# A fused attention and feed-forward kernel: the order of every engine's work taken from written-out lists, and copies and casts moved between VectorE, ScalarE and GpSimd

## The chip, the core and the metric

The kernel runs on one core of one Trainium2 chip. Its time is the device time of one execution in microseconds (us). The engines are TensorE (PE in the profile; its weight loads are PEld), VectorE (DVE), ScalarE (ACT), GpSimd (POOL) and SyncE (SP), whose queue issues nearly all DMAs here.

## What is computed

A recurrent attention (4 batches, 8 heads, 768 steps, head size 48) is followed by a feed-forward layer over its 3072 rows. Cut to what matters:

```
for t in range(S):
    state = alpha[:, :, t, :, None] * state + einsum('bhd,bhe->bhde', k[:, :, t], v[:, :, t])
    y[:, :, t] = einsum('bhd,bhde->bhe', q[:, :, t], state)
x = y.transpose(0, 2, 1, 3).reshape(B * S, H * D)      # 3072 x 384
h = x @ w_in                                           # 384 x 2048
r = maximum(h, 0)
out = (s * (r * r) + b) @ w_out                        # 2048 x 384
```

## The kernel before

**Tiling.** The 3072 rows are 24 blocks of 128 steps, six to a batch. Attention is done a block at a time in chunked form. Blocks 0 to 5 come in three pairs, loaded in 384 KB pieces (`load_pair`); blocks 6 to 23 are single, in 192 KB pieces (`load_block`). Each has four loads, a (alpha), q, k and v. Below, a7 means the a load of block 7. There are four pair-sized buffers for each of the four, so a load of block n waits until block n-8 has been used.

**Steps of a block.** Names ending in `_1` forms (st1_...) are those of single blocks, the others those of pairs.
- ln: ACT takes the logarithm of a; cum: PE sums it along the steps; exp: ACT makes the decay and its inverse.
- vcast: v to bf16 (L524 for pairs, L740 for single blocks). For pairs 0 and 1, PE also reorders v (V) and ACT copies it (Vcopy, L543).
- qb, kb: DVE multiplies q and k by the decays (L554, L562, L746).
- T: PE transposes them (8 instructions), and Tcopy copies the result from PSUM (128x1024 bf16, L582 or L584 for pairs, two copies a pair; L764 for single blocks). Blocks 13 to 23 have a DMA transpose in place of both (Tdma).
- KV: PE; then the state: sfirst (DVE, first block of a batch, two instructions, L618), or t1 (DVE, L626) and snew (POOL, two instructions, L633).
- A: PE (L658); mask: DVE (L672); y: PE (L689, L697); yevac: ACT (L791).
- yT: PE transposes y (3 instructions, L796), yTcopy puts it in place (L808 DVE, L810 ACT); or one DMA transpose (yTdma, L813).

**Feed-forward.** The blocks form groups of 1, 1, 2, 2, 2, 4, 2, 2, 2, 2, 4. There are 96 units of the first product, mm1(0) to mm1(95) (PE, L834), each 512 columns of PSUM, each followed by relu (ACT, L843) and square (DVE, L855). Units 0 to 7 belong to blocks 0 and 1 and have 12 matmuls each, units 8 to 23 to blocks 2 to 5 and have 6. The second product is 100 quads of four matmuls, mm2(0) to mm2(99) (PE, L867), four quads a block and eight half quads for the last block. The last quad of a block is followed by oevac (DVE) or, for blocks 0 to 5, by oscale (ACT) and obias (POOL), and by ostore (SP).

**Weights.** Four pieces of w_in (w0 to w3) and then four of w_out (o0 to o3), 768 KB each, pass through the same four staging tiles `wst`, and each is cast in two halves on ACT or POOL (`cast_w_in(i, e)`, `cast_w_out(i, e)`). So o0 can't be loaded before both halves of w0 are cast. DVE also sums the w_out pieces (colsum, L427 and L435) for the bias term.

**PSUM.** Two banks hold `a_ps`; six more are handed out step by step: at most three hold results of mm1, two those of mm2, and two each those of cum, T and so on.

**What sets the order.** Each step is told to a planner by `op(engine, duration, priority, function, ...)` with what it reads and writes. `Schedule.run` plays the steps forward with these planned durations: whenever an engine is free it takes the ready step of the lowest priority number, where the number has an offset per kind of step (`KIND`) and per block (`BLOCK`), and loads are ranked by the string `LOADS`. `emit` then writes the instructions in the order of the planned begins. On the chip, each engine works through its own instructions strictly in that order, and a step whose input is late holds up all that stands behind it. Gaps of PE that are planned before 36 us are filled with matmuls of zeros (`warm`, L1137).

**Who does what.** Small lists say it: `POOL_CASTS` and `WIN_CASTS` (halves of w_out and w_in cast on POOL, the rest on ACT), `POOL_V` (pairs whose v is cast on POOL), `DVE_YC` (yTcopy on DVE, the rest on ACT), `PE_T` and `PE_Y` (single blocks transposed by PE rather than by DMA), `N_ACT_T` (pairs whose first Tcopy is on ACT).

Of the kernel before, what the change touches and what calls it, by code (L numbers as in the profile page):

```python
# [15 lines left out]
UNIT = 1.62  # L16
# [4 lines left out]
POOL_CASTS = [1, 3, 5, 7]  # L21
CASTP = -400.0
W_HW = True
WIN_CASTS = [0, 2, 3, 5, 7]
A2 = [0, 1, 2, 5, 8, 9, 10]
POOL_V = [0, 1, 2, 4]
DVE_VC = [6]
DVE_YC = [0, 2, 4, 6, 7]
NIN = 4
PE_T = [6, 7, 8, 9, 10, 11, 12]  # L30
PE_Y = [6, 7, 8, 9, 10, 11, 13]
# [3 lines left out]
N_ACT_T = 1  # L35
# [3 lines left out]
KIND = {'bias_copy': 2.5, 'bias_mm': 0.0, 'bias_mul': 2.75, 'cast_w_in': 0.0, 'cast_w_out': -0.625, 'colsum_add': 0.75, 'colsum_fold': -10.75, 'colsum_part': 1.625, 'mm1': 0.0, 'mm2': 3.375, 'obias': -11.25, 'oevac': 0.0, 'oscale': 9.75, 'relu': 0.0, 'square': 0.0, 'st1_KV': 18.75, 'st1_T': 0.0, 'st1_Tcopy': -5.625, 'st1_cum': -3.375, 'st1_exp': 0.75, 'st1_ln': 20.875, 'st1_qb': -2.25, 'st1_vcast': 0.0, 'st_A': -8.625, 'st_A2': 0.0, 'st_KV': -16.625, 'st_T': -0.5, 'st_Tcopy': 0.25, 'st_V': 10.625, 'st_Vcopy': 11.0, 'st_bl': 0.125, 'st_blexp': 0.0, 'st_cum': 0.25, 'st_exp': 0.0, 'st_kb': -19.0, 'st_ln': -0.875, 'st_mask': 0.0, 'st_qb': 0.0, 'st_sfirst': 0.0, 'st_snew': 0.0, 'st_t1': -1.625, 'st_vcast': -1.75, 'st_y': 0.0, 'st_yT': -0.375, 'st_yTcopy': 6.125, 'st_yevac': 6.125}  # L39
BLOCK = [-7.0, 0.375, -15.875, -1.125, 2.625, -0.5, -14.75, 5.375, -21.25, 0.125, 0.0, 0.875, 0.0, 0.0, -2.875, -13.75, 1.0, 2.375, 1.25, 3.625, -3.125, 18.375, 1.125, 6.375, 0.75, -0.625, 0.0, -7.75, 0.625, -21.375, -0.5, 3.25, 2.375, 2.5, 9.25]  # L40

LOADS = 'o1 a0 a1 q0 k0 v0 k1 q1 w0 v1 w1 w2 w3 o0 a2 k2 q2 v2 o2 o3 a7 k9 a9 v6 v7 a6 k7 q9 q6 k6 a8 q14 k8 k10 a10 a11 q7 k20 q10 q8 v9 v8 q15 a12 q11 v17 v11 q13 v13 k11 v10 q12 q16 a14 v12 a13 k14 k12 k17 k15 q23 k13 a15 v15 k16 q20 v16 q18 a16 a21 v14 q17 v18 a17 v21 a19 v23 a18 k19 k21 k18 a22 a20 k22 v20 v19 q19 v22 q21 a23 q22 k23'


class Schedule:
# [11 lines left out]
    pool_busy = 0.0  # L57
# [11 lines left out]
    def op(self, eng, dur, prio, fn, *args, r=(), w=(), lat=0.1, dma=None, take=(), drop=None, blk=None):  # L69
        me = len(self.ops)  # L70
        prio += KIND.get(fn.__name__, 0.0)
        if blk is not None:
            prio += BLOCK[blk]
        deps = set()
        for x in r:
            if x in self.writer:
                deps.add(self.writer[x])
        for x in w:
            if x in self.writer:
                deps.add(self.writer[x])  # L80
            deps.update(self.readers.get(x, ()))
        for x in r:
            self.readers.setdefault(x, []).append(me)
        for x in w:
            self.writer[x] = me
            self.readers[x] = []
        if drop is not None:
            self.drops[drop] = self.drops.get(drop, 0) + 1
        self.ops.append((eng, dur, prio, fn, args, deps, lat, dma, take, drop))

    def run(self):
        n = len(self.ops)
        end = [None] * n
        begin = [None] * n
        left = [len(o[5]) for o in self.ops]
        users = [[] for _ in range(n)]
# [3 lines left out]
        free = {}  # L100
        ready = {}
        for i, o in enumerate(self.ops):
            free.setdefault(o[0], {"POOL": 6.9, "DVE": 4.5}.get(o[0], 0.7))
            ready.setdefault(o[0], [])
            if not left[i]:
                ready[o[0]].append((0.0, i))
# [4 lines left out]
        soft = 0.0  # L111
        queue = 4.0
        flying = []
        todo = n

        def since(u):
            a = 0.0
            for d in self.ops[u][5]:
                same = self.ops[d][0] == self.ops[u][0]
                x = end[d] + (0.0 if same and u_eng(u) == "PE" else self.ops[d][6])  # L120
                a = max(a, x + (0.0 if same and self.ops[d][7] is None else self.HOP))
            return a

        def u_eng(u):
            return self.ops[u][0]

        def may(b, i, at):
            return b or at > self.warm_until

        def start(a, i):  # L130
            take = self.ops[i][8]
            if not take:
                return a
            if held[take[0][0]] + len(take) > self.most[take[0][0]]:
                return None
            free_banks = sorted(v for b, v in idle.items() if may(b, i, max(a, v)))
            return max(a, free_banks[len(take) - 1]) if len(free_banks) >= len(take) else None

        while todo:
            best = None  # L140
            for e, items in ready.items():
                at = [(s, i) for a, i in items if (s := start(a, i)) is not None]
                if not at:
                    continue
                t = max(free[e], min(at)[0])
                _, i = min((self.ops[i][2], i) for s, i in at if s <= t + 1e-9)
                if best is None or t < best[0]:
                    best = (t, e, i)
            t, e, i = best
            ready[e] = [x for x in ready[e] if x[1] != i]  # L150
            eng, dur, _, _, _, _, lat, dma, take, drop = self.ops[i]
            begin[i] = t
            if dma is None:
                if eng == "DVE" and self.ops[i][3].__name__ in self.shared:
                    dur += 0.9 * min(dur, max(0.0, self.pool_busy - t))
                free[e] = end[i] = t + dur
                if eng == "POOL":
                    self.pool_busy = end[i]
            elif eng == "POOL":
                free[e] = t + dur  # L160
                at = max(t + 3.2, soft)
                soft = end[i] = at + 1.1 * dma + (1.2 if soft < at < queue else 0.0)
                flying = [x for x in flying if end[x] > at]
                for x in flying:
                    end[x] += dma
                queue = max(queue, at) + dma
                for e2, items in ready.items():
                    ready[e2] = [(since(x), x) for _, x in items]
            else:
                queue = max(t + self.LEADS.get(self.ops[i][3].__name__, 1.8), queue) + dma  # L170
                end[i] = queue
                flying.append(i)
                free[e] = max(t + dur, queue - self.AHEAD)
            for x in take:
                b = min(
                    (b for b in idle if may(b, i, max(t, idle[b]))), key=lambda b: (idle[b], -b)
                )
                del idle[b]
                self.bank[x] = b
                held[x[0]] += 1  # L180
            if drop is not None:
                until[drop] = max(until.get(drop, 0.0), end[i] + lat + self.HOP)
                drops[drop] -= 1
                if not drops[drop]:
                    idle[self.bank[drop]] = until[drop]
                    held[drop[0]] -= 1
            todo -= 1
            for u in users[i]:
                left[u] -= 1
                if not left[u]:  # L190
                    ready[u_eng(u)].append((since(u), u))
# [29 lines left out]
def kernel(  # L221
# [356 lines left out]
    def st_Tcopy(m, x):  # L578
        dst = qkT_of(m)[:, :, x].rearrange("a c u j -> a c (u j)")
        src = t_of(m, x).rearrange("a c u j -> a c (u j)")  # L580
        if x < 1 and m < N_ACT_T:
            nc.scalar.activation(out=dst, in_=src, func=AF.Copy)  # L582
        else:
            nc.vector.tensor_copy(out=dst, in_=src)  # L584
# [39 lines left out]

    def st_t1(n):
        nc.vector.tensor_tensor(  # L626
            out=t1_sb[n % 2], in0=p_of(n), in1=s_sb[(n - 1) % 4], op=ALU.add
        )

    def st_snew(n):  # L630
        for e in range(2):
# [3 lines left out]
                in0=t1_sb[n % 2][rows, :, cols],  # L635
# [103 lines left out]
    def st1_vcast(n):  # L739
        nc.gpsimd.tensor_copy(  # L740
            out=vb_sb[n // 2 % 2][:, n % 2],
            in_=block_in(v_in, n).rearrange("a h d -> a (h d)"),
        )
# [19 lines left out]
    def st1_Tcopy(n):  # L763
        nc.vector.tensor_copy(  # L764
            out=qkT1_of(n).rearrange("a x p t -> a (x p t)"),
            in_=t1_of(n).rearrange("a x p t -> a (x p t)"),
        )
# [197 lines left out]
    def pair_ops(pm):  # L965
# [40 lines left out]
        if pm < N_PAIR_T:  # L1006
            for x in range(2):
                tb = ("T", 2 * pm + x)
                op("PE", 0.46, t, st_T, pm, x, r=src[x], w=[tb], lat=0.27, take=[tb], blk=c0)
                eng, dur = ("ACT", 0.92) if x < 1 and pm < N_ACT_T else ("DVE", 0.6)  # L1010
# [13 lines left out]
    def state_ops(n, t, pb):  # L1024
        s0, s1 = ("S", (n - 1) % 4), ("S", n % 4)
        bl = ("bl", n // 2 % 2, n % 2)
        if n % NCH == 0:
# [35 lines left out]
    def block_ops(n):  # L1063
# [10 lines left out]
        op("POOL", 0.6, t, st1_vcast, n, r=[("v", *ii)], w=[("vb", *j)], blk=n)  # L1074
# [4 lines left out]
        if n in PE_T:  # L1079
            op("PE", 0.46, t, st1_T, n, r=qk, w=[("T", n)], lat=0.27, take=[("T", n)], blk=n)  # L1080
            op("DVE", 0.6, t, st1_Tcopy, n, r=[("T", n)], w=[("qkT", *j)], drop=("T", n), blk=n)
# [94 lines left out]
```

## Time and profile before

| | |
|---|---|
| median of 7 runs | 185.66 us (184.99 to 186.12) |
| profiled execution | 185.71 us, span 183.9 us |
| PE busy | 173.8 us (94%), 1807 matmuls |
| DVE busy | 138.6 us (75%) |
| ACT busy | 111.0 us (60%) |
| POOL busy | 55.0 us (30%) |
| DMA | 34.36 MB, mean 187 GB/s |
| first mm1 begins | 22.1 us |
| last matmul ends | 180.9 us |

The profiled execution's span lies 1.8 us under its own time; that time is within 0.05 us of the median. PE's busy time is no measure of what it gets done, since its ends are modelled: what counts is how far apart matmuls start. Back to back, a unit of mm1 takes 0.66 us, a quad of mm2 0.65 us, eight transposes 0.45 us.

### The profile page before, as it was taken

To read this page: it belongs to the slowest core of one execution; us is meant where nothing else is said; L and a number is where in the kernel's file an instruction comes from. 1 tells how busy PE (TensorE), PEld (TensorE's weight loads), DVE (VectorE), ACT (ScalarE), POOL (GpSimd) and SP (SyncE) were. 2 spreads that over 40 slices of the span, in tenths; PEclk is the share of its full clock that TensorE was granted. 3 is DMA by queue.
4 is the path that set the end of the run, shared out by engine and by line. 5 is a ranking of instruction groups with operands and counts; after the bars stand their busy time and mean duration, and the time that the engine had idled before them with its cause. 6 is when DMAs were issued, how large, how long until landed. Compare 5 with 4: busy or idle time off the path is not lost.

```text
span 183.9 us, 4689 instructions
## 1 busy us (share of the span) xinstructions
PE 173.8 (94%) x1807; PEld 123.0 (67%) x1807; DVE 138.6 (75%) x253; ACT 111.0 (60%) x237; POOL 55.0 (30%) x103
## 2 busy tenths in 40 slices
PE   7496899899999999999999999999999999999993
PEld 5274787677776778775455867877866687554572
DVE  6069959999999997899886583887879966356241
ACT  2582499769778548675857755688743165459100
POOL 7843749262064236410211272011232310000000
PEclk9969999999999999999999999999999999999999
DMA  4999999979999998999869997988993552201022
GB/s 98 264 310 347 391 361 259 325 175 212 191 219 248 215 212 185 218 208 214 220 135 198 215 174 178 228 176 178 183 218 95 118 150 46 87 2 43 4 86 87
DMA packets 111495, 34.36 MB, mean 187 GB/s; under 512 B 104432, under 2 KB 109936, under 8 KB 111472
## 3 DMA queue, kind: packets, MB, share of 16 engines
q1 hardware_dynamic: 111184, 34.06, 78.8%
q8 instruction: 14, 0.23, 0.5%
q14 instruction: 9, 0.07, 0.1%
q10 hardware_dynamic: 288, 0.00, 0.1%
HBM read 25.17 MB, written 4.72 MB: 162 GB/s over the span
## 4 chain that ended last, share of the span: by engine, by line
PE 64%; DVE 17%; SPq 7%; DMA 5%; issue 4%; ACT 1%; ACTq 0%; DVEq 0%
PE bank L867 28%; PE bank L834 26%; SPq L372 5%; DMA wst<-in_moe_w_in_dram 5%; DVE gt L855 4%; DVE qk L746 3%; PE a_ps L658 2%; DVE am L672 2%; PE bank L697 2%; DVE colsum L435 2%; DVE colpart L427 2%; SPq L399 2%; PE bank L689 1%; PE bank L778 1%; PE bank L713 1%
## 5 line engine op out<-in xcount | busy, mean ns | idle before, releaser
L867 PE MATMUL bank<-w_out_bf,gt 128*128 128x384 bf16 (+1 forms) x400 | 72.0, 319 | 0.4 <-DVE gt L855 0.4
L834 PE MATMUL bank<-xd,w_in_bf 128*128 128x256 bf16 (+2 forms) x528 | 71.1, 282 | 0.5 <-ACT binv L511 0.3
L843 ACT ACTIVATE r<-bank 128x512 bf16<-128x512 f32 x96 | 56.1, 600 | 24.6 <-PE bank L834 11.1
L834 PEld LDWEIGHTS <-w_in_bf 128*128 128x128 bf16 x528 | 46.2, 98 | 16.0 <-issue 0.8
L855 DVE TENSOR_TENSOR gt<-r 128x512 bf16<-128x512 bf16 x96 | 44.3, 475 | 16.6 <-ACT r L843 16.0
L867 PEld LDWEIGHTS <-gt 128*128 128x128 bf16 x400 | 36.2, 97 | 19.7 <-DVE gt L855 0.5
L740 POOL CAST vb<-v_in 128x384 bf16<-128x384 f32 x18 | 10.2, 571 | 49.3 <-DMA v_in<-in_v_dram 18.0
L633 POOL TENSOR_TENSOR s_st<-t,blast 64x192 bf16<-64x192 bf16 x32 | 19.3, 602 | 18.9 <-DVE t L626 15.9
L877 DVE SCALAR_TENSOR_TENSOR o_sb<-bank,s_col,bias_w 128x384 f32<-128x384 f32 (+1 forms) x19 | 11.3, 594 | 13.6 <-PE bank L867 13.5
L672 DVE TENSOR_TENSOR am<-a_ps,mask_one 128x1024 bf16<-128x1024 f32 x14 | 17.1, 1220 | 2.1 <-PE a_ps L658 1.9
L791 ACT ACTIVATE yn<-bank 128x384 bf16<-128x384 f32 x24 | 11.8, 493 | 11.2 <-PE bank L697 11.0
L728 ACT ACTIVATE b_s<-bank 128x384 f32<-128x384 f32 x18 | 8.9, 492 | 7.3 <-PE bank L718 6.4
L746 DVE TENSOR_TENSOR qk<-q_in,b_s 128x384 bf16<-128x384 f32 x18 | 12.1, 674 | 0.9 <-ACT b_s L728 0.8
L706 ACT ACTIVATE la<-a_in 128x384 bf16<-128x384 f32 x18 | 9.4, 521 | 2.2 <-DMA a_in<-in_alpha_dram 2.2
L746 DVE TENSOR_TENSOR qk<-k_in,binv 128x384 bf16<-128x384 f32 x18 | 10.4, 583 | 0.0
L626 DVE TENSOR_TENSOR t<-bank,s_st 128x384 bf16<-128x384 f32 x16 | 8.8, 549 | 1.5 <-PE bank L778 1.0
L901 POOL TENSOR_TENSOR o_sb<-o_sb,bias_w 128x384 f32<-128x384 f32 x6 | 6.3, 1059 | 9.4 <-DVE bias_w L461 6.2
L728 ACT ACTIVATE binv<-bank 128x384 f32<-128x384 f32 x18 | 8.9, 497 | 0.0
L1137 PE MATMUL bank<-zeros_bf 128*128 128x256 bf16 x36 | 7.4, 359 | 1.1 <-DVE zeros_bf L298 1.1
L697 PEld LDWEIGHTS <-am 128*128 128x128 bf16 x192 | 7.1, 96 | 1.6 <-DVE am L672 1.2
L658 PEld LDWEIGHTS <-qkT 64*128 64x128 bf16 x192 | 5.5, 94 | 3.4 <-issue 2.1
L689 PE MATMUL bank<-s_st,qkT 128*128 128x96 bf16 x80 | 6.7, 206 | 0.3 <-DVE xd L808 0.3
(84 smaller groups left out, 181.4 us busy)
## 6 DMA issues: line engine op xcount, KB each, us to landing
out_dram<-o_sb SPq DMA_DIRECT2D x23, 192.0 KB, 2.2
a_in<-in_alpha_dram SPq DMA_DIRECT2D x18, 192.0 KB, 3.8
k_in<-in_k_dram SPq DMA_DIRECT2D x18, 192.0 KB, 4.0
v_in<-in_v_dram SPq DMA_DIRECT2D x18, 192.0 KB, 3.8
q_in<-in_q_dram SPq DMA_DIRECT2D x18, 192.0 KB, 3.7
wst<-in_moe_w_in_dram SPq DMA_DIRECT2D x4, 768.0 KB, 8.6
wst<-in_moe_w_out_dram SPq DMA_DIRECT2D x4, 768.0 KB, 7.4
a_in<-in_alpha_dram SPq DMA_DIRECT2D x3, 384.0 KB, 6.2
```

The source lines that it names most:

```text
L633: nc.gpsimd.tensor_tensor(out=s_sb[n % 4][rows, :, cols], in0=t1_sb[n % 2][rows, :, cols], in1=blast(n)[rows].unsqueeze(2).to_broadcast([6 ...
L672: nc.vector.tensor_tensor(out=dst, in0=src, in1=mk.unsqueeze(1).to_broadcast([128, dst.shape[1], 128]), op=ALU.mult,)
L697: nc.tensor.matmul(out=y_of(n)[:, 48 * h : 48 * h + 48], lhsT=am_sb[n % 2][:, h % 2, h // 2, :], rhs=v[:, 48 * h : 48 * h + 48], start=(h ...
L728: nc.scalar.activation(out=(binv_sb if inv else b_sb)[n // 2 % 2][:, n % 2].rearrange("a h d -> a (h d)"), in_=cb[:, 0 : H * D], func=AF.E ...
L740: nc.gpsimd.tensor_copy(out=vb_sb[n // 2 % 2][:, n % 2], in_=block_in(v_in, n).rearrange("a h d -> a (h d)"),)
L746: nc.vector.tensor_tensor(out=qk1_of(n)[:, x, :, 0:D], in0=block_in((q_in, k_in)[x], n), in1=(b_sb, binv_sb)[x][n // 2 % 2][:, n % 2], op= ...
L791: nc.scalar.activation(out=yn_sb[n // 2 % 2][:, n % 2], in_=y_of(n), func=AF.Copy)
L834: nc.tensor.matmul(out=hp[:, i * n : (i + 1) * n], lhsT=w_in_bf[:, kk, 128 * j : 128 * (j + 1)], rhs=xd_sb[g % 3][:, kk, 0:n], start=(kk = ...
L843: nc.scalar.activation(out=r_sb[w % 2], in_=bank("h", w), func=AF.Relu)
L855: nc.vector.tensor_tensor(out=dst, in0=r, in1=r, op=ALU.mult)
L867: nc.tensor.matmul(out=bank("o", i)[:, cols], lhsT=gt_sb[:, slot, j, :], rhs=w_out_bf[:, j, cols], start=(j == 0), stop=(j == NJ - 1),)
L877: nc.vector.scalar_tensor_tensor(out=out_sb[i % NOUT][:, cols], in0=bank("o", i)[:, cols], scalar=s_col, in1=bias_w[:, cols], op0=ALU.mult ...
```

## The change

**The lists.** `KIND`, `BLOCK` and the choice by priority go. A dictionary `ORDER` holds, for each of the five engines, the numbers of all its steps (the number of a step is its place in the sequence of `op` calls) in the order in which the engine is to do them. `run` only walks the lists, gives out PSUM banks and works out the planned begins as before.

**Who does what:**

```diff
-POOL_CASTS = [1, 3, 5, 7]
+POOL_CASTS = [0, 1, 3, 5, 7]
-WIN_CASTS = [0, 2, 3, 5, 7]
+WIN_CASTS = [1, 4, 6]
-POOL_V = [0, 1, 2, 4]
-DVE_VC = [6]
-DVE_YC = [0, 2, 4, 6, 7]
+POOL_V = [0]
+ACT_V1 = [6, 17, 18, 22, 23]
+ACT_T1 = [6, 7, 8, 9, 10, 11]
+DVE_VC = []
+DVE_YC = [0, 2, 3, 8, 9, 10, 11]
-PE_Y = [6, 7, 8, 9, 10, 11, 13]
+PE_Y = [7, 8, 9, 10, 11, 13]
-N_ACT_T = 1
+ACT_T = [0, 2, 3, 4]
+ACT_S = [0]
...
+ORDER = {
+    "SP": """
+        31 35 34 32 33 37 36 38 3 0 6 9 39 12 40 16 42 41 21 26 43 351 47 211 45 44 46 49 48 395
...
+    "POOL": """
+        51 56 79 81 2 7 156 10 14 13 18 23 158 28 230 301 308 359 381 200 111 366 403 388 207
...
         for _ in range(n):
             best = None
-            for e, items in ready.items():
...
+            for e in engines:
...
+                i = lists[e][place[e]]
+                assert self.ops[i][0] == e
+                if left[i]:
+                    continue
+                a = max(known[i], free[e])
...
+    def st_scopy(n):
+        nc.scalar.activation(out=scratch(), in_=p_of(n), func=AF.Copy)
+
+    def scratch():
+        return out_sb[NOUT - 1].rearrange("a (p e) -> a p e", p=NP)
...
+        dst = vb_sb[n // 2 % 2][:, n % 2]
+        src = block_in(v_in, n).rearrange("a h d -> a (h d)")
+        if n in ACT_V1:
+            nc.scalar.activation(out=dst, in_=src, func=AF.Copy)
+        else:
+            nc.gpsimd.tensor_copy(out=dst, in_=src)
...
+        if n in ACT_T1:
+            nc.scalar.activation(out=dst, in_=src, func=AF.Copy)
+        else:
+            nc.vector.tensor_copy(out=dst, in_=src)
...
+        if n in ACT_S:
+            op("ACT", 0.37, t, st_scopy, n, r=[pb], w=[("os", NOUT - 1)], drop=pb, blk=n)
+            op("POOL", 1.2, t, st_snew, n, r=[("os", NOUT - 1), bl], w=[s1], blk=n)
+        elif n % NCH == 0:
```

In words: of the pair Tcopies, three more are on ACT (both of pair 1, one of pair 2); of the seven single ones, six (blocks 6 to 11) are on ACT and one stays on DVE. The first state of block 0 is no longer two DVE instructions but a copy on ACT (scopy) and two instructions on POOL. v is cast on ACT for pairs 1 and 2 and for blocks 6, 17, 18, 22 and 23, before on POOL. Of w_in, five halves are cast on ACT and three on POOL (before three and five), of w_out three and five (before four and four). Block 6's y is transposed by DMA instead of by PE. `LOADS`, `UNIT` and the priorities no longer decide anything. No other arithmetic is changed.

**The lists, translated** (from the step numbers; on the left the order in which the planner before emits, to the same point):

| engine | before | after |
|---|---|---|
| SP, loads | a0 a1 q0 k0 v0 k1 q1 w0 v1 w1 w2 w3 o0 o1 a2 k2 q2 v2 o2 o3, the DMAs of Vdma(2), a7 k9 a9 v6 v7 a6 k7 q9 q6 k6 | a0 a1 v0 q0 k0 k1 q1 v1 w1 w0 w2 w3 a2 o0 q2 o1 v2 k2 o2 o3 a6 a8 a7, those of Vdma(2), k6 q6 v6 k7 q7 a10 v7 k8 |
| DVE, from kb of pair 1 | kb(1) twice, Tcopy(0,1), sfirst(0), qb(1) twice, Tcopy(1,1), t1(1), mask(0), Tcopy(1,0), mask(1) in two halves, mask(2), yTcopy(0) | kb(1) twice, Tcopy(0,1), qb(1) twice, mask(0), mask(1) in two halves, t1(1), half of mask(3), yTcopy(0) |
| ACT, from the first Tcopy | Tcopy(0,0), Vcopy(0) twice, cast_w_in(0,1), yevac(0), Vcopy(1,0), yevac(1), cast_w_in(2,0), Vcopy(1,1), yevac(2), yTcopy(1), relu(0) | Vcopy(0,1), Tcopy(0,0), Vcopy(0,0), scopy(0), vcast(1), Tcopy(1,1), Tcopy(1,0), cast_w_in(1,0), yevac(0), cast_w_in(1,1), yevac(1), Vcopy(1,0), cast_w_in(0,0), Vcopy(1,1), yTcopy(1), cast_w_in(2,1), relu(1), relu(0) |
| PE, around the first units | y(0), A(2) and A(3), V(1,0), yT(0), y(1), V(1,1), y(2), yT(1), mm1(0), mm1(1), mm1(2), KV(1) | y(0), A(2) and A(3), y(1), V(1,0), yT(0), V(1,1), yT(1), KV(1), mm1(1), mm1(0), y(2), mm1(4), mm1(2) |
| PE, first transposes of single blocks | T(9) ahead of mm1(16), then T(6), T(7), T(10), T(8), T(11), T(12) | T(6) ahead of mm1(16), then T(7), T(8), T(9), T(10), T(11), T(12) |

Later in the lists, cum and ln of single blocks stand well ahead of where they were (cum(18) is 144th on PE, before 204th), and neighbouring mm1 units often swap places. The last 15 steps of PE are quads of mm2 in both.

## The prediction, made before the changed kernel was run

> **What bounds the kernel now.** I read the page first (parts 1, 2 and 4), then the chain of waits in order of time, then busy times by stretch, then the waits, then groups by line and form.
>
> ```profile
> PE   7496899899999999999999999999999999999993
> DVE  6069959999999997899886583887879966356241
> ACT  2582499769778548675857755688743165459100
> DMA  4999999979999998999869997988993552201022
> ```
>
> PE looks full nearly throughout, ACT has room, and DVE and DMA are near their limit in the first half. The chain says where the halves meet: until 61.7 us it is made of DVE steps (squares, qk products, column sums, masks), with the w_in loads before 22 us; from then to 180.9 it is PE alone.
>
> ```profile
> 61.70 0.84 DVE qk L746
> 62.59 0.62 PE bank L757 x8
> ...
> 170.43 10.45 PE bank L867 x80
> 180.91 0.42 DVE o_sb L877
> ```
>
> So the end is fixed by how much PE work is done by 62.6 us. By stretch (from:to, length; busy us of PE, PEld, DVE, ACT, POOL; clock, DMA share, GB/s):
>
> ```profile
> 8.80:22.10 13.30, 11.13 (x154) 8.31 (x153) 11.44 (x21) 6.90 (x16) 6.39 (x9) 0.87 1.06 345
> 22.10:62.60 40.50, 39.25 (x481) 30.34 (x478) 37.74 (x63) 32.54 (x72) 17.60 (x22) 1.00 0.99 250
> 62.60:180.90 118.30, 118.27 (x1146) 80.99 (x1146) 85.89 (x161) 68.17 (x145) 23.72 (x39) 1.00 0.72 152
> ```
>
> In 22.1 to 62.6 PE did 192 matmuls of L834, which are 24 units at 0.66 us (15.8), 68 of L867, 17 quads at 0.65 (11.1), and 221 of attention and bias, at their back-to-back pitch 10.6 us. That is 37.5 of 40.5 us: **3.0 us were lost** there. In the 118.3 us after it nothing that a wait row shows was lost. Before 22.1, the first units wait for their inputs. DVE was 93% busy in the middle stretch, ACT 80%.
>
> **The change, part by part.**
>
> *Copies from DVE to ACT.*
>
> ```profile
> L764 DVE COPY qkT<-bank 128x1024 bf16<-128x1024 bf16 x7 | 4.8, 680 | 0.2 <-PE bank L757 0.2
> L582 ACT ACTIVATE qkT<-bank 128x1024 bf16<-128x1024 bf16 x1 | 1.1, 1119 | 0.0
> ```
>
> Nine copies (three of pairs, six of single blocks): DVE loses 9 x 0.68 = 6.1 us, ACT gains 9 x 1.12 = 10.1. The Trainium skill speaks against such a move: "ScalarE: Activation LUTs", in its rules for kernel authors, says to use VectorE for simple elementwise work, up to about three times as fast in bf16. By that, the nine would cost ACT 9 x 3 x 0.68 = 18.4 us, and ACT would reach 133 us from this edit and the next. The row says 1.65 times for this very tile, read from PSUM. I take the row.
>
> *The rest.* DVE also loses sfirst(0) (2 x 0.35) and gains two yTcopies net (2 x 0.34): minus 6.1 us in all, 138.6 to 132.5. ACT gains scopy (0.49, as the Vcopy of that shape), two pair casts of v (2 x 0.85, nearest row ln of that shape at 844 ns), five single ones (5 x 0.52, ln at 521), one w half net (0.85), and loses three yTcopies (1.5): plus 4.1, so 111.0 + 10.1 + 4.1 = 125 us. POOL loses two pair casts (1.8), five single ones (2.9) and one w half net (0.8), and gains snew(0) (1.2): minus 4.3. So although one more half of w_out is cast there, GpSimd casts 22 tiles instead of 30. PE loses three transposes (0.17 us); SP gains one DMA transpose.
>
> *POOL against DVE.* The "SBUF" page of the Trainium skill ("SBUF — State Buffer", the rule on the shared port pair) says a DVE step with two SBUF inputs and a GpSimd step that reads SBUF exclude each other for the whole instruction. In this trace the 65 squares with no POOL work beside them took 0.42 us, the 31 with some 0.59. By the rule 4.3 us less on POOL could free up to 4.3 us of DVE; by the trace, where DVE lost some 10 us (31 x 0.17 on squares, 11 x 0.26 on L746, the rest on L554 and column sums) to 46 us of POOL work, 1 us. I take 1; the end doesn't hang on it once DVE is relieved.
>
> *Head start.* Ahead of yTcopy(0), which mm1(0) needs, DVE does from 12.64 us on (start to start) before: kb 0.95, Tcopy 0.60, sfirst 0.71, qb 0.95, Tcopy 0.60, t1 0.47, mask 1.13, Tcopy 0.60, masks 1.20, mask 1.13: 8.3, so at 21.1. After: without the sfirst, two Tcopies and mask(2), but with half of mask(3): 5.9, so from 18.6. ACT then decides. Vcopies, Tcopies, scopy and vcast, 5.0 us from 11.7 on, are done before w1 comes: the casts of w0 and w1 began at 16.7 and 20.0, one pair piece and w1 apart; after, w1 is loaded ahead of w0 and behind that pair piece, so it lands some 1.4 us behind the old w0, at 18.1. From there cast 0.75, yevac(0) 0.38, cast 0.75, yevac(1) 0.38, yT(1) 0.3 and KV(1) 0.5 put mm1(1) at 21.1, and mm1(0), after its own cast, at 21.8. The first unit was at 22.1. By the pitches above, the lists have 7.8 us of PE work ahead of it before, 7.9 after: **1.1 us** gained. The bounds are 0 (casts on ACT late) and 2.4 (DVE's whole saving).
>
> *The stretch to 62.6.* Adding durations down the lists, DVE's work to the end of square(15) falls from 36.7 to 28.1 us: sfirst(0) and three Tcopies are gone (2.5), and behind it now stand a column sum, two adds and the fold, four qk products of later blocks, a yTcopy and a square (6.4), while one yTcopy (0.3) came ahead. It ended at 50.9. On ACT, work to relu(15) is 30.9 against 29.4; to relu(31) 61.5 against 47.9, which ended at 78.7, 31 us of it idle. ACT's first relu ends near 23.5, with 14.9 us of its list done; relu(31) then can't end before 70.1, 8.6 us ahead of what it was. So ACT has cover, if thin: 46.6 us of work in what was 55. Loads are the other limit, DMA share is 0.99. Before, the first T of a single block (T(9)) needed 12.6 MB of loads with 33.1 us of PE work ahead of it (its list at the pitches above); after, T(6) needs 12.0 MB at 31.8. That is 0.6 MB, 2.8 us at 212 GB/s, for 1.3 us of PE work: loads allow 1.5 us more lead, and for T(7), with as many loads as T(9) had, 35.4 - 33.1 = 2.3 us. So of the 3.0 us lost I take half back: **1.6 us**, bounds 0 and 3.0.
>
> *New waits.* v casts on ACT now stand ahead of relus; yTdma(6) stands on SP ahead of q10, k11, a14 and waits for yevac(6). It costs nothing if the loads issued before it (the queue runs some 4 us ahead of landing) last; else about 1 us of loads for T(10). bias_mm moves 17 places back on PE, and with it the first obias; behind that on POOL stands snew(8), due only at y(9). After 62.6 PE's order has lost its old zero of waits. For all this nothing in the trace gives a price; nearest are PE's own waits before (0.2 to 0.8 us each), bounds 0 and 3: I take two small ones, **0.7 us** lost; a gain is excluded, since PE loses nothing there now.
>
> *Tail.* The last mm2 quads, two evacuations and stores are as before: 0.
>
> Sum on the profiled execution: 185.7 - 1.1 - 1.6 - 0.2 + 0.7 = 183.5; its time equals the median within 0.05.
>
> **The rivals.**
>
> *Full gain* (0.15): ACT and loads both keep up, the 3.0 us vanish and nothing new comes: 185.7 - 1.1 - 3.0 - 0.2 = 181.4. For it: DVE's 8.6 us less by square(15). Against: DMA share 0.99 up to 62 us.
>
> *Slower: ACT's queue held by v* (0.26). In-order ACT has relus behind seven v casts.
>
> ```profile
> POOL vb L740 <- DMA v_in<-in_v_dram: 18.0, 8, 4.1
> ACT r L843 <- PE bank L834: 11.1, 19, 1.2
> ```
>
> On POOL 8 of 18 casts waited, 2.25 us each, hidden there since POOL was 30% busy. On ACT some three of the seven would wait: PE goes on for two units in free banks (1.3 us) and then stalls, 0.95 us each, 2.9 in all, while nothing of the 3.0 us comes back. It decides as soon as a v lands over 1.3 us after ACT reaches its cast. Time: 185.7 - 0.2 - 1.1 + 2.9 = 187.3. Against it: the loads are now in the order of the blocks, so v6 and v7 land with their own q and k.
>
> *No difference* (0.13): the loads set the pace, PE waits at T(6) to T(13) for what it gained, and the bound just changes its name: 185.7 - 0.2 = 185.5. For it: DMA at 0.99 to 1.06; against: the 0.6 MB above. That the change doesn't do what it says belongs here too: its casts on GpSimd fall, so no gain can come from more of them.
>
> **How the numbers follow.** Forecast 0.46 (183.5; own range 182.3 to 184.8), full gain 0.15, no difference 0.13, slower 0.26. A change under 0.3% (0.6 us) can't be told from none here. Faster: 0.46 + 0.15 = 0.61; same 0.13; slower 0.26. The range goes from just under the full gain, 181.2, to the slower rival's 187.3.
>
> **What would show it.** Right: first L834 matmul at 21 us; DVE under 90% in 22 to 62, ACT over 90%; the chain turning to PE alone some us earlier; PE's L867 and L834 without waits later; DVE 131 to 133, ACT near 125, POOL near 51 us. Wrong: ACT waiting on v_in with PE waiting on ACT r; PE waits after 62; SP waiting on yevac(6) with loads behind; or the first unit no earlier than 22.

## The result and the profile after

| | before | after |
|---|---|---|
| median | 185.65 us (34 runs) | 183.72 us (13 runs, 182.89 to 185.28) |
| profiled execution | 185.71 us, span 183.9 | 184.39 us, span 182.6 |
| first mm1 begins | 22.1 us | 21.27 us |
| last matmul ends | 180.9 us | 179.5 us |

The ratio of after to before is 0.9895, interval 0.9871 to 0.9919: 1.9 us faster, against a forecast of 183.5 us. Some executions of a kernel fall into a slower state: medians here are of all runs, ratios and their intervals of the others alone. The profiled execution of after is 0.7 us above its median. The changed kernel was run once more beside the last experiments (184.39 us where before took 186.41, ratio 0.9872 [0.9815, 0.993]); that run's profiled execution took 183.55 us, so I read both. Line numbers of after are 30 to 45 higher: mm1 L834 is now L874, mm2 L867 is L907, Tcopy L764 is L805 on ACT, vcast L740 is L781 on POOL and L779 on ACT; in the experiments they differ from these by one to three.

Busy time of after by engine, and its busy tenths in 40 slices, from the page:

```profile
PE 174.0 (95%) x1797; PEld 122.0 (67%) x1797; DVE 130.6 (72%) x244; ACT 120.1 (66%) x252; POOL 49.5 (27%) x97
...
DVE  6079748979699996989776697366896983454332
ACT  2578999979799879957976652846535056666200
...
DMA  4999999977899899999999989997985972000323
```

DVE's unbroken nines of before are gone, ACT's row is now the fuller one up to 60 us, and DMA has a seven and an eight at 41 to 50 us where it had nines. PE is busy for the same 174 us: it does the same work in a shorter span. By stretch, in the columns used before:

```profile
22.10:62.60 40.50, 39.62 (x498) 31.07 (x496) 33.72 (x60) 37.05 (x80) 15.65 (x21) 1.00 0.94 231
62.60:179.50 116.90, 116.52 (x1107) 78.56 (x1105) 82.11 (x158) 67.62 (x146) 22.13 (x36) 1.00 0.73 159
```

In 22.1 to 62.6 DVE went from 37.74 to 33.72 us, ACT from 32.54 to 37.05, and PE ran 498 matmuls in place of 481. The chain of waits, in order of time (start, us, what), turns to PE for good later than before:

```profile
43.34 4.71 DMA k_in<-in_k_dram
...
48.14 0.56 DVE qk L784
...
63.82 0.48 DVE qk L784
64.34 0.62 PE bank L795 x8
...
71.71 0.41 ACT la L742
72.12 0.50 ACT r L883
72.66 0.32 PE bank L749
```

The DVE stretch is shorter (8% of the chain, 17% before): it began near 27 us and now runs from 48.1, where a load of k lands, to 64.3. The loads ahead of it and SP, which issues them, are 23% of this chain (12% before), but 3% of the chain of after's second run, so nothing is built on that. A logarithm on ACT at 72 us stands in the chain as a new late step. And the waits of after (engine and line, what it waited for, us in total, times, longest):

```profile
POOL vb L781 <- DMA v_in<-in_v_dram: 38.0, 9, 11.6
...
ACT vb L779 <- DMA v_in<-in_v_dram: 1.8, 2, 1.1
...
PE bank L818 <- ACT vb L779: 0.5, 1, 0.5
PE bank L560 <- ACT yn L831: 0.5, 1, 0.5
```

The same kind of wait costs PE nothing here on POOL, where it adds up to 38 us, and 0.5 us of PE time on ACT, where it adds up to 1.8.

To see where the time came from I took, for each step of PE's list, its start minus the PE work that stands ahead of it in that list (at the back-to-back pitches). Before's value less a kernel's own is the kernel's lead:

| PE work done, us (time) | after | after, second run | h1, early DVE undone | h2 | h3 | e3 | e2 |
|---|---|---|---|---|---|---|---|
| 7.9, the first unit (21) | 1.0 | 1.4 | -0.5 | 0.4 | 1.3 | 0.6 | 1.1 |
| 20 (34) | 2.3 | 2.9 | 1.4 | 2.3 | 2.4 | 2.5 | 2.1 |
| 32 (47) | 2.3 | 2.9 | 1.4 | 2.3 | 2.4 | 1.9 | -0.9 |
| 42 (57) | 1.4 | 2.2 | 0.8 | 2.2 | 1.4 | 1.7 | -2.2 |
| 58 (75) | 1.1 | 2.1 | 0.0 | 1.7 | 1.2 | 1.8 | -6.6 |
| 160 (178) | 1.2 | 2.1 | -0.9 | 1.8 | -0.5 | 1.7 | -6.4 |

All of it is won before 34 us, and 0.8 to 1.2 us is given back between 47 and 75 us, in small waits. From there on the lead of after is constant. The profiled executions of h1 and h3 took 1.0 and 1.6 us more than their medians, so of their columns the early rows count.

Between the first unit and 34 us PE loses some 2.3 us in before and 1.0 in after, in small waits on several engines. The waits of 22 to 40 us name only 0.9 us of before's loss; here they are, and then all of after's:

```profile
PE bank L867 <- DVE gt L855: 0.4, 1, 0.4
PE bank L834 <- ACT binv L511: 0.3, 1, 0.3
PE bank L834 <- ACT r L843: 0.2, 1, 0.2
```

```profile
PE bank L836 <- ACT r L883: 0.2, 1, 0.2
```

### The profile page after: what moved, and what is told of

Its sections match the earlier page's. It is cut to its first block, busy times and chain, and to the rows that moved or that the text cites. A ratio compares the mean times of both kernels' runs of the same rounds, so it can differ in the third digit from the quotient of the medians.

```text
span 182.6 us, 4621 instructions
## 1 busy us (share of the span) xinstructions
PE 174.0 (95%) x1797; PEld 122.0 (67%) x1797; DVE 130.6 (72%) x244; ACT 120.1 (66%) x252; POOL 49.5 (27%) x97
## 4 chain that ended last, share of the span: by engine, by line
PE 61%; SPq 14%; DMA 9%; DVE 8%; issue 3%; POOL 1%; ACT 1%; ACTq 0%; POOLq 0%; DVEq 0%
PE bank L907 28%; PE bank L874 25%; DMA wst<-in_moe_w_in_dram 6%; SPq L402 5%; SPq L409 5%; DMA k_in<-in_k_dram 3%; DVE qk L784 2%; DVE gt L895 2%; DVE am L708 2%; PE bank L733 2%; PE a_ps L694 2%; PE bank L725 1%; SPq L429 1%; SPq L579 1%; PE bank L818 1%
## 5 line engine op out<-in xcount | busy, mean ns | idle before, releaser
L874 PE MATMUL bank<-xd,w_in_bf 128*128 128x256 bf16 (+2 forms) x528 | 73.2, 282 | 0.1
L907 PE MATMUL bank<-w_out_bf,gt 128*128 128x384 bf16 (+1 forms) x400 | 72.7, 319 | 0.0
L874 PEld LDWEIGHTS <-w_in_bf 128*128 128x128 bf16 x528 | 45.6, 98 | 15.5 <-issue 0.3
L907 PEld LDWEIGHTS <-gt 128*128 128x128 bf16 x400 | 36.5, 97 | 19.4
L669 POOL TENSOR_TENSOR s_st<-t,blast 64x192 bf16<-64x192 bf16 x32 | 17.9, 560 | 35.0 <-DVE t L662 26.8
L781 POOL CAST vb<-v_in 128x384 bf16<-128x384 f32 x13 | 7.7, 594 | 45.9 <-DMA v_in<-in_v_dram 38.0
L784 DVE TENSOR_TENSOR qk<-k_in,binv 128x384 bf16<-128x384 f32 x18 | 11.0, 610 | 1.6 <-ACT vb L779 1.6
L784 DVE TENSOR_TENSOR qk<-q_in,b_s 128x384 bf16<-128x384 f32 x18 | 10.8, 601 | 1.6 <-DMA q_in<-in_q_dram 1.6
L764 ACT ACTIVATE b_s<-bank 128x384 f32<-128x384 f32 x18 | 9.1, 523 | 1.8 <-PE bank L754 1.6
L764 ACT ACTIVATE binv<-bank 128x384 f32<-128x384 f32 x18 | 9.0, 514 | 1.3 <-PE bank L754 1.3
L452 POOL CAST w_out_bf<-wst 128x768 bf16<-128x768 f32 x5 | 5.5, 1120 | 7.9 <-DMA wst<-in_moe_w_out_dram 7.9
L584 DVE TENSOR_TENSOR qk<-q_in,b_s 128x384 bf16<-128x384 f32 x6 | 3.8, 659 | 5.2 <-DMA q_in<-in_q_dram 5.2
L1182 PE MATMUL bank<-zeros_bf 128*128 128x256 bf16 x29 | 6.2, 374 | 1.1 <-DVE zeros_bf L328 1.1
```

What stands on the lines that cost most here:

```text
L669: nc.gpsimd.tensor_tensor(out=s_sb[n % 4][rows, :, cols], in0=(scratch() if n in ACT_S else t1_sb[n % 2])[rows, :, cols], in1=blast(n)[row ...
L764: nc.scalar.activation(out=(binv_sb if inv else b_sb)[n // 2 % 2][:, n % 2].rearrange("a h d -> a (h d)"), in_=cb[:, 0 : H * D], func=AF.E ...
L784: nc.vector.tensor_tensor(out=qk1_of(n)[:, x, :, 0:D], in0=block_in((q_in, k_in)[x], n), in1=(b_sb, binv_sb)[x][n // 2 % 2][:, n % 2], op= ...
L874: nc.tensor.matmul(out=hp[:, i * n : (i + 1) * n], lhsT=w_in_bf[:, kk, 128 * j : 128 * (j + 1)], rhs=xd_sb[g % 3][:, kk, 0:n], start=(kk = ...
L907: nc.tensor.matmul(out=bank("o", i)[:, cols], lhsT=gt_sb[:, slot, j, :], rhs=w_out_bf[:, j, cols], start=(j == 0), stop=(j == NJ - 1),)
```

## The experiments

Theory: DVE's in-order queue held back the first units; taking four early steps out of it, three ahead of the first mask and one just behind, makes most of the gain, and waits behind ACT and behind loads give part of it back. Rivals: the loads set the pace; or DVE's total work does; or some other place in the new orders does. Kernels of one group ran on one chip, each ratio is to runs of the kernel before there (186.6, 185.6 and 186.4 us).

**e1, who does what, without the new orders.** The planner of before, with the lists of after:

```
-POOL_V = [0, 1, 2, 4]
+POOL_V = [0]
+ACT_V1 = [6, 17, 18, 22, 23]
+ACT_T1 = [6, 7, 8, 9, 10, 11]
-N_ACT_T = 1
+ACT_T = [0, 2, 3, 4]
+ACT_S = [0]
...
```

> Who does what as after the change (nine copies, the first state, the casts), but the order from the old planner with its old priorities and load ranks. My theory: the shorter DVE work ahead of the first unit and in the first 60 us is what counts, but the old priorities were set for another division of the work and w0 is loaded before w1 again, so ACT, with 10 us more to do, is now late: about 185.0 us, first unit near 22. Rival 'the division of work is the whole gain': 183.7 us. Rival 'the order is the whole gain': 185.7 us or slower.

Measured: 189.48 us, 1.0125 [1.0068, 1.0182]. Its first unit began at 21.50 us, but with 0.4 us less PE work ahead of it in this list: a lead of 0.2 us. So the division by itself shows hardly any of the head start, and then more is lost. The chain of this kernel:

```profile
28.27 5.33 DMA v_in<-in_v_dram
...
33.68 0.84 ACT vb L529
34.53 0.38 ACT binv L514
...
35.02 0.66 PE bank L575 x8
```

ACT reaches the cast of v of pair 2, waits until its load has landed, and the decay behind it, and so PE's transposes, come late. This is the mechanism of the prediction's slower rival, ACT held by a v that hasn't landed, with a decay rather than a relu behind it. Later it costs again (at 81.2 us ACT had waited 1.85 us for a load of alpha). The division makes the kernel slower by 1.2% unless the orders are made for it.

**e2, the copies back on VectorE.** After's orders, nine Tcopies put back on DVE, each a step or two behind its qk product; nothing else moved:

```
-ACT_T = [0, 2, 3, 4]
-ACT_T1 = [6, 7, 8, 9, 10, 11]
+ACT_T = [0]
+ACT_T1 = []
```

> The lists of the changed kernel, but the nine copies of transposes are done by DVE again, each a step or two behind the qk product that it needs. My theory: two of the nine lie ahead of yTcopy(0) (plus 1.2 us on DVE, first unit near 22.2) and the other seven put 4.2 us back on DVE before 70 us, so the lead is gone: 185.5 us, and up to 187 since the lists were made for the copies on ACT. Rival 'the order is the whole gain': 183.7 us.

Measured: 192.15 us, 1.0293 [1.0249, 1.0338]. My expectation for the start, near 22.2 us, was wrong: the first unit began at 21.17 us, between after's two profiles, though the first mask was at 16.07 instead of 15.71. A smaller delay can't be read from one profile: in the six profiled executions whose orders are those of after up to there (after twice, e3, h3, a1, a2) the first unit began between 20.35 and 21.68 us. The loss begins with pair 2's copies. Chain of this kernel:

```profile
35.54 0.69 DVE qkT L612
...
38.77 0.65 DVE gt L893
39.42 0.46 DVE colsum L455
...
41.24 0.61 DVE qkT L612
...
41.90 0.40 PE a_ps L692 x8
```

From 35.5 us PE runs on DVE's heels, and the copy that the attention product waits for stands behind squares and a column sum. So ACT's copies after 34 us are needed in these orders. That they are worth 4% anywhere is not shown: the places were mine, not made for it.

**e3, v of block 6 loaded earlier.** After, with one load moved on SP's queue, since the lead falls by 0.65 us where ACT waits 1.15 us for it:

```
 SP order
-a6 a8 a7 Vdma(2) k6 q6 v6 ...
+a6 v6 a8 a7 Vdma(2) k6 q6 ...
```

> The changed kernel with the load of v6 put three loads earlier on SP, right behind a6. In the changed kernel KV(6) waited on PE for the cast of v6 on ACT, which had waited 1.15 us for the load; PE's lead over the old kernel fell there from 2.3 to 1.6 us. My theory: that wait vanishes, 0.5 to 0.65 us are kept: 183.1 us, unless later waits swallow it. Rival 'the loads' pace sets the time': k6 and q6 now come 1 us later and T(6) waits instead: 183.7 us or slower.

Measured: 184.71 us, 0.9895 [0.9853, 0.9938], the ratio of after itself. The wait on v6 is gone and T(6), whose q and k now land later, starts 0.4 to 0.7 us late in its place. Inconclusive as an improvement.

**e4, the DMA transpose of block 6 later on SP.** After, with yTdma(6) moved eight places back, ahead of ostore(3), to let q10, k11 and a14 pass:

```
 SP order
-k10 yTdma(6) q10 k11 a14 ... ostore(3)
+k10 q10 k11 a14 ... yTdma(6) ostore(3)
```

> The changed kernel with the DMA transpose of block 6's y moved eight places back on SP, behind the loads up to a12. In the changed kernel SP stood 2.2 us there, waiting for the evacuation of y on ACT, with q10 and k11 behind it, and the DMA share was 0.85. My theory: it frees about 1 us of loads for T(10), whose qk product waited; PE lost 0.5 us there: 183.3 us. Rival 'ACT, 95% busy there, sets the pace': no change, 183.7 us.

Measured: 191.43 us, 1.0243 [1.0195, 1.0292], where I had expected a gain of 0.4 us over after. Waits of PE in this kernel, and SP's queue:

```profile
PE bank L873 <- DMA xd<-yn: 5.7, 1, 5.7
```

```profile
63.06 2.13 SPq L408 DMA_DIRECT2D a_in<-in_alpha_dram  x2
65.30 1.32 SPq L852 DMA_TRANSPOSE xd<-yn  x1
```

In after it was issued at 56.75 us and PE needed its result near 61.6; eight places on SP are 8.5 us. The step that I had read as being in the way was just in time. Nor did SP wait there for ACT, as I had thought: in after the evacuation of block 6's y ended at 54.76 us, 2 us before SP came to the transpose, and the 2.19 us are the issue itself.

**b1 and a1, less work on VectorE.** Before and after, leaving out three of the four column sums of w_out and the adds (bias term incomplete), 6.3 us of DVE work:

```
 def colsum_part(i, more):
+    if more: return
 def colsum_add():
+    return
```

> The kernel before, leaving out three of the four column sums of w_out and the three adds (so the bias term of the output is not the reference's): 6.3 us less work on DVE between 30 and 48 us. My theory: DVE is what the old kernel's PE loses its 3.0 us to in that stretch, so about half of it comes back: 184.2 us (minus 1.5), at most minus 3. Rival 'the loads' pace is the old bound': no change, 185.7 us.

> The changed kernel with the same work left out of DVE (three column sums and three adds, the bias term wrong). My theory: with the copies on ACT, DVE no longer holds PE up before 46 us; only a late chain over qk products and squares at 48 to 64 us could still gain: 183.4 us (minus 0.3). Rival 'DVE is still the bound': minus 1 us or more, 182.7 us or less.

Measured: 185.3 us, 0.9973 [0.9948, 0.9998], for before's; 183.97 us, 0.9911 [0.9876, 0.9945], for after's, which gains nothing. Row of before's version by stretch:

```profile
22.10:62.60 40.50, 39.01 (x476) 30.03 (x473) 30.62 (x56) 32.24 (x72) 16.40 (x21) 1.00 0.95 242
```

DVE was busy for 30.6 us of the 40.5 instead of 37.7, more relief than the change gives there, and PE got through no more. Its lead over before at 34 us is 0.2 us, with 2.4 us of the column sums' work gone by then. I had expected 184.2 us. So what held PE in the middle was not the sum of DVE's work there. The column sums begin after the first unit, so this run says nothing on DVE's queue ahead of it; h1 does.

**b2 and a2, fewer loads.** Before and after, without the loads of q and v of blocks 8 to 11 (stale values are used), 1.6 MB:

```
 def load_block(...):
+    if n in (8, 9, 10, 11) and (dst is q_in or dst is v_in): return
```

> The kernel before, with the q and v loads of blocks 8 to 11 left out (those blocks are computed from older data in the same buffers): 8 of 192 KB, some 8 us of DMA work between 45 and 65 us. My theory: the loads come second to DVE there, so the old kernel gains little: 185.2 us (minus 0.5). Rival 'the loads' pace is the old bound': minus 1.5 us or more, 184.2 us or less.

> The changed kernel with the same eight loads left out. My theory: of the 1.2 us of lead that PE gives back between 46 and 73 us, the waits on q, k and v loads are the larger part and vanish (v6 itself comes no earlier): minus 0.6 us, 183.1 us. Rival 'ACT, 95% busy there, sets the pace': no change, 183.7 us. Rival 'the loads alone set the pace after the change': minus 1.2 us or more, 182.5 us.

Measured: 186.35 us, 1.0048 [1.0017, 1.0079], and 184.7 us, 0.9958 [0.9936, 0.998]. Row of before's version:

```profile
45.00:65.00 20.00, 19.80 (x228) 14.66 (x226) 19.85 (x36) 14.52 (x37) 7.47 (x9) 1.00 0.85 184
```

The DMA share there fell from 1.01 to 0.85 and no time was gained: the loads of that stretch were not the bound, in either kernel. Earlier loads weren't taken out. That both are slower by half a per cent was not expected; in after's version SP has no loads left to issue and stands 2.5 us at yTdma(6), and PE waits 0.9 us for a state sum on DVE. For before's I have no cause.

**h1, VectorE's early steps put back.** After, with the early steps that had left DVE, or moved back on it, in their old places and nothing else changed: the state product sfirst(0) (on ACT and POOL in after), one copy of pair 1 and t1(1) ahead of mask(0), and the other copy right behind it. ACT and POOL lose what DVE takes back:

```
 DVE order
-Tcopy(0,1) qb(1,1) qb(1,0) mask(0) mask(1,0) mask(1,1) t1(1)
+Tcopy(0,1) sfirst(0) qb(1,1) qb(1,0) Tcopy(1,1) t1(1) mask(0) Tcopy(1,0) mask(1,0) mask(1,1)
```

> The changed kernel with VectorE's four early steps as before: the first state product, both copies of pair 1's transposes, and the first state sum ahead of the first mask, all on VectorE; every other place in the orders stays. Theory one, the head start comes from VectorE's shorter queue ahead of the first mask: that mask started at 17.06 us before and 15.71 us after, with a copy (0.69), two state products (0.71) and a state sum (0.55) ahead of it before. Put back, the first mask starts near 16.8 and the first unit of the first layer near 22.0 instead of 21.27; about 0.7 us later to the end, 184.4 us. Theory two, ScalarE's queue sets the start of the first unit (the wait of 0.5 us for the evacuation of y ahead of the last V transpose), as the run with the copies on VectorE suggested, where the first mask was late and the first unit was not: the unit stays at 21.2 to 21.4 and the time at 183.7 us, or a little under since ScalarE has less to do.

Measured: 185.87 us, 0.9975 [0.9934, 1.0016], where the unchanged after beside it has 0.9872. DVE in time (start, us), first of h1, then of after's second run:

```profile
14.79 0.72 DVE L647 TENSOR_TENSOR s_st<-bank,blast 64x192 bf16<-64x192 f32 x2 [0.16 <-PE bank L629]
15.54 1.03 DVE L583 TENSOR_TENSOR qk<-q_in,b_s 128x384 bf16<-128x384 f32 x2
16.60 0.69 DVE L613 COPY qkT<-bank 128x1024 bf16<-128x1024 bf16 x1
17.21 0.55 DVE L661 TENSOR_TENSOR t<-bank,s_st 128x384 bf16<-128x384 f32 x1
17.68 1.22 DVE L707 TENSOR_TENSOR am<-a_ps,mask 128x1024 bf16<-128x1024 f32 x1
```

```profile
14.46 1.33 DVE L583 TENSOR_TENSOR qk<-q_in,b_s 128x384 bf16<-128x384 f32 x2
15.71 1.21 DVE L707 TENSOR_TENSOR am<-a_ps,mask 128x1024 bf16<-128x1024 f32 x1
```

The first mask is 1.97 us later, and the first unit, in the same two kernels:

```profile
22.78 1.40 PE L873 MATMUL bank<-xd,w_in_bf 128*128 128x128 bf16 x22
```

```profile
20.84 1.51 PE L873 MATMUL bank<-xd,w_in_bf 128*128 128x128 bf16 x24
```

It is 1.94 us later, and 1.1 us later than the latest of the six executions named under e2. This is the strongest result: the two intervals lie apart, if only just, h1's includes 1, and by the medians 1.5 us of after's 2.0 hangs on four steps of DVE (by the ratios 1.0% of 1.3%). The lead at 34 us is smaller by 0.9 to 1.5 us. What h1 loses behind that in the table is partly another thing, a wait of PE of 1.3 us at 60 us for a v that landed late. Which of the four steps carries it isn't shown: in e2 the two copies alone moved the first mask by 0.36 us and the first unit by -0.1 or 0.3 us, less than the scatter; the state product and the state sum weren't put back alone.

**h2, the place of y(2).** After, with PE's y(2) ahead of mm1(1) and mm1(0), as before had it:

```
 PE order
-KV(1) mm1(1) mm1(0) y(2) mm1(4)
+KV(1) y(2) mm1(1) mm1(0) mm1(4)
```

> The changed kernel with one step of TensorE moved: the output product of block 2 ahead of the first two units of the first layer, where the kernel before had it, instead of behind them. Theory one, this place carries the head start: in the changed kernel's profile the mask that the product needs ends at 21.67 us, so the first unit would begin near 22.1 us instead of 21.27, and of the 0.8 us some 0.3 is the product itself, done earlier: 0.4 to 0.5 us lost to the end, 184.2 us. Theory two, the units that follow wait anyway for their weights, so the loss is made good within 5 us: 183.7 us, with the same lead from 30 us on.

Measured: 184.19 us, 0.986 [0.9797, 0.9922]. The first unit began at 22.21 us with a lead of 0.4, and at 34 us the lead was that of after's first profile again, as theory two has it. By the ratio no loss is seen to the end, though with 4 runs the interval leaves room for the 0.4 us of theory one. It also warns against reading the start of the first unit as the head start; the lead in PE work is what lasts.

**h3, three late waits taken away.** After, with the cast of v of block 6 two places later on ACT, KV(6) two later and cum(12) one later on PE:

```
 ACT  -vcast(6) yTcopy(4) yTcopy(5)     +yTcopy(4) yTcopy(5) vcast(6)
 PE   -KV(6) mm2(13) mm1(16)            +mm2(13) mm1(16) KV(6)
 PE   -cum(12) mm2(21)                  +mm2(21) cum(12)
```

> The changed kernel with three steps moved to take away two of its late waits: ScalarE's cast of v of block 6 behind the two copies that follow it, TensorE's state product of block 6 two steps later, and TensorE's cumulative sum of block 12 one step later, behind the second-layer unit that follows it. Theory one, these waits are on the path and nothing else is late behind them: TensorE lost 0.65 us at 47 to 49 us and 0.65 us near 72 us, so up to 1.3 us is to be had; I expect half, 183.1 us, a ratio of 0.986 to the kernel before, with a lead at 80 us of 1.8 us instead of 1.15. Theory two, as with v6 loaded earlier, the next late step (the transposes of block 6, which wait for VectorE's products, or the attention product of block 6, which waits for ScalarE's copy) takes the place of each wait: 183.7 us.

Measured: 184.59 us, 0.9881 [0.9822, 0.9939]; no gain over after beside it. The wait at 48 us is gone (PE runs almost without a gap from 46.72 to 49.3 below), and A(6), T(7) and A(7) behind it start late instead: PE in time,

```profile
46.72 1.46 PE L906 MATMUL bank<-w_out_bf,gt 128*128 128x384 bf16 x8
48.02 0.82 PE L873 MATMUL bank<-xd,w_in_bf 128*128 128x256 bf16 x6
48.67 0.33 PE L817 MATMUL bank<-vb,qk 128*128 128x96 bf16 x4
48.94 0.40 PE L693 MATMUL a_ps<-qkT 64*128 64x128 bf16 x8
...
50.12 0.62 PE L794 MATMUL bank<-ident_bf,qk 128*128 128x128 bf16 x8
50.88 0.32 PE L748 MATMUL bank<-la,U_one 128*128 128x384 bf16 x1
```

A gap of 0.2 us ahead of 50.12 and of 0.3 ahead of 50.88, 0.4 more at 53.2: 0.9 us in all, more than was removed. No run beat the changed kernel by more than its interval.

**h4, after once more.**

> The changed kernel itself, unchanged, on the same chip as the three others, so that they can be compared with it: a ratio of 0.9895 to the kernel before, 183.7 us, first unit at 21.2 to 21.4 us. Its first profiled execution took 184.39 us, more than its median; if that was chance, the lead of TensorE over the kernel before ends nearer to 1.9 us here than to 1.3.

Measured as told above: first unit 20.84 us, earlier than I had allowed, and the lead ends at 2.1 us. The gain in median and the lead in this profile agree; the first profile was a poorer execution of the same lists.

## Why the prediction was right

**The bound.** "The end is fixed by how much PE work is done by 62.6 us" held in this: the lead is constant from 75 us on. One sign that I had named failed: the chain turned to PE alone at 72.7 us in after's first profile, not some us before 62.6 (at 63.8 in the second). What misled was the picture of DVE and DMA near their limit in the first half. b1 took 7 us from DVE and b2 took the DMA share from 1.01 to 0.85, and neither gained over 0.3%. DVE's fullness in the middle was not the cause; for the head start, what stood in its queue ahead of 18 us was.

**The head start, 1.1 us.** 1.0 in one profile, 1.4 in the other. The two-part reasoning, DVE's queue first and then ACT, is borne out: with DVE's steps put back (h1) the unit falls 1.94 us back, so that queue decided before; in after's second run the chain into the first unit is ACT's copy, casts and evacuations,

```profile
16.50 1.02 ACT qkT L611
17.53 0.64 ACT w_in_bf L439
18.17 0.47 ACT yn L830
...
19.26 0.50 ACT yn L830
```

and PE waits for the last of them ahead of its last V (0.5 us in the first profile, L560 above), so ACT decides now. In the first profile its cast of w1 began at 17.85 us, for 18.1 forecast, and the first unit at 21.27, for 21.1; in the second 17.43 and 20.84.

**The stretch, 1.6 us.** The lead grew by another 1.35 us (first profile) and 1.5 (second). The size came out, but not by the reasoning, so that is luck. In h1, with the head start gone, the lead still grows by 1.9 us up to 34 us, so this term doesn't come from the four early steps (a later start finds more inputs ready, which is part of its 1.9); nor does it show when DVE has less to do (b1, 0.2 us at 34 us). It is several small waits of before that the new orders don't have, and no run isolates one. I had it as half of what was lost up to 62.6 us, with the loads as the brake; it was all won by 34 us, and the loads of 45 to 65 us were no brake (a2).

**New waits, 0.7 us.** 1.2 and 0.8 us, in three places: KV(6) on the v6 that ACT casts, T(10) on its qk product, cum(12) behind ACT. Kind and place of the first are the slower rival's, at one cast, not three: ACT waited 1.8 us on v in all. I had said that PE's waits would come with ACT's r; they came with v itself.

**yTdma(6).** I had it wait for yevac(6) and cost nothing, or about 1 us of loads. SP was held 2.19 us by the issue, not by that wait, and PE's only wait at the T(10) behind it was 0.2 us, for a qk product. e4 shows the side that I had not seen, 5.7 us where it comes late.

**Copies and counts.** The row for the copy, 1119 ns, was a little high: ACT's copies took 1018 to 1041 ns in after,

```profile
L805 ACT ACTIVATE qkT<-bank 128x1024 bf16<-128x1024 bf16 x6 | 6.2, 1041 | 0.0
```

1.5 times the 680 ns of DVE. The Trainium skill ("ScalarE: Activation LUTs", rules for kernel authors) gives its factor, up to about three, for single-source bf16 operations in DVE's 4x mode; it doesn't say it of a copy that reads PSUM, so the 18.4 us that the prediction drew from it stretched the page. With that factor the seven copies of the middle stretch would have given ACT 7 us more to do where it had 3.5 us idle. ACT came to 120.1 us, not 125. The added durations were right: ACT's records sum to 127.1 us before and 141.7 after, 14.6 more for 14.2 forecast. But back-to-back records of ACT overlap, by 16.2 us before and 21.6 after, and busy time counts an overlap once. DVE came to 130.6 us (132.5 forecast), POOL to 49.5 (51).

**POOL beside DVE.** I took 1 us of relief for DVE. On the squares there was none: beyond 0.42 us each they lost 5.3 us before and 5.9 after. And what the prediction read as a mild slowdown looks like the exclusion that it quotes: of the squares that began while a GpSimd step ran, 17 of 21 before and 21 of 25 after ended 0.27 to 0.29 us after that step's end, with up to 1.22 us on the record instead of 0.42. One before and three after ended inside the step, against the rule, on records of GpSimd that are rough. No run tried what this is worth.

**The rivals.** Full gain, a lead of 4.1 us, was never reached: 2.9 us in the second profile, before the new waits. "No difference" falls with the result; of its reason, that the loads set the pace, b2 and a2 exclude the loads of 45 to 65 us. The slower rival is a real mechanism that the new orders avoid: in e1, under the old planner, it made the kernel 1.2% slower.

What stays open: how much of the head start is the state product's, the state sum's and the copies', which of the small waits up to 34 us makes the second term, and what slows b2.

## What to carry to other kernels

Look at what stands in an engine's queue ahead of the first step that another engine waits for, not at how full the engine is: here four early steps of DVE were worth some 1.5 us, and 6.3 us of its later work 0.5 us (0.0 to 1.0). A change of who does what can't be judged apart from the order: the same division was 1.2% slower under the old order and is 1.05% faster under its own. When waits of half a microsecond are all that is left, taking one away shows the next one behind it, so measure the lead over the whole program, not the wait.

## What the runs showed of the hardware

- A DMA share of 0.99 to 1.01 was no bound: with 1.6 MB fewer it was 0.85, and the time didn't fall.
- A DMA transpose of one block's y (128x384) held SP's queue for 1.2 to 2.2 us (12 of them in after, half under 1.23), and its result was there 2.3 to 4.5 us after the issue began (median 3.1).
- A square on DVE that began while a GpSimd step ran mostly ended 0.27 to 0.29 us after that step (17 of 21 before, 21 of 25 after), where it takes 0.42 us alone.
- The same program gave a first unit at 21.27 and 20.84 us in two profiled executions, with 0.6 us between their leads at 34 us and 0.9 at the end: one profile isn't enough for steps of half a microsecond. Over six profiled executions with the same orders up to there the first unit ranged from 20.35 to 21.68 us.
